# RWKV-7 attention into a SiLU layer: one ScalarE instruction for each gate, three places for w, a freer order of the weight pieces, and the scores of k in a step of their own

## The chip, the cores and the metric

The kernel runs on one core of one Trainium2 chip. The metric is the device time of one execution in microseconds. TensorE is called PE, VectorE DVE, ScalarE ACT, GpSimd POOL, and SyncE SP, as in the profile.

## What is computed

The attention part runs an RWKV-7 state over 768 tokens for 4 batches of 8 heads with 40 channels. Its output y, with the heads side by side, is the input x of a layer with 2048 hidden units:

```python
for t in range(S):
    y[:, :, t] = np.einsum('bhd,bhde->bhe', rt, state)
    Sa = np.einsum('bhde,bhe->bhd', state, at)
    state_decay = state * wt[:, :, None, :] - np.einsum('bhd,bhe->bhde', Sa, bt)
    state = state_decay + np.einsum('bhd,bhe->bhde', vt, kt)
...
h = x @ w_in
g = h * (1.0 / (1.0 + np.exp(-h)))
return (g @ w_out).astype(np.float32)
```

Everything is float32. x is 3072 x 320, w_in 320 x 2048, w_out 2048 x 320.

## The kernel before

The 768 tokens go in 12 **chunks** n of 64; the four batches form two **units** m of two batches each, so that there are 24 units k = 2n + m. Within a chunk the token recurrence is replaced by matrix products and the inverse of a lower triangular matrix. For each unit the program runs:

- **prepare** (`pre`): a running scan over w (L308) and its reciprocal (L309) on DVE, the scaling of a, b and k by them on POOL (L315, L316, L322) and two checks on ACT (L325, L326); then the scores of a and b (`pm`, L261, masked by DVE into `sb`, L269), which go to memory and come back as `mi` for the inverse. At the end of its `scores` step a unit starts the load of w for the next one (`load_w`), into the tile `w0`.
- **invert**: the inverse of the diagonal blocks, one row after another on DVE, each row a product (L380, `tmp`) and a sum (L387, `XI`). Blocks of 16 rows for chunks 0 to 3, blocks of 32 rows from chunk 4 on; from chunk 2 on two chunks are inverted at a time, during the end of the chunk before them. The result goes through memory (`xd`) to the tiles `XT`, one for each of the two chunks, which DVE transposes (L424). `merge` completes the inverse on PE (`pq`, L433 or L482, and L499).
- **chain**, which carries the state and so binds each chunk to the one before it: `keys` (transposes of k, L556 and L557), `right` (first the scores of k by `keyed`: PE L285 and the masked DVE copy L290 into `a`; then the right-hand sides `pr`, L568), `solve` (L588, L606), `read` (`pl`, L656, and the masked DVE copy `vl`, L664), `write` (`pgy`, L678 and L688; the new state `GV` by DVE L701 and L705; the output `yx`, L710, which ACT's queue sends to memory as `xs`) and `turn` (the transposed state `GT`, L631).

The hidden layer (`moe`) takes the x of two chunks. Their `xs` comes back as the tile `xt`. A step of `first` makes two 128-wide slices of h for 512 columns (256 columns for chunks 0 and 1): four calls of L753 and two of L758 into two PSUM banks `ph` of three that the layer has; ACT writes the sigmoid into `sg` (L761) and DVE multiplies (L762) into `gts`. A step of `second` is 16 calls of L767 into `po`, which DVE or ACT adds into `ot` (L776, L779). Half of the hidden units is done by eight first and four second steps, then the other half. In the trace a matmul call in float32 counts as two instructions.

The weights come in a form that the kernel makes into float32 itself, in 40 **pieces** of 256 columns: DVE steps L178, L179, L187, L189 and L190 (about 0.3 to 0.5 us each) with ACT steps L180 to L182 between them.

What sets the order: the steps of two or three lists are woven (`weave`) in proportion to their lengths, and a scheduler then orders each engine's instructions by its own estimate of times; every engine runs its list in that order. `in_order` ties an instruction to the one before it on a named line ("vector", "moe", "scalar", "sync"), so that the scheduler keeps this order. Before, the scans and reciprocals of chunks 0 to 3 and the pieces 0 to 11 are tied in the line "vector", with the rows of the first two inverses.

Of the kernel before, what the change touches and what calls it, by code (L numbers as in the profile page):

```python
# [41 lines left out]
def kernel(  # L42
# [15 lines left out]
    nc = tc.nc  # L58
# [44 lines left out]
    XI = XIf[:, 0 : 32 * 32].rearrange("p (s t) -> p s t", s=32)  # L103

    w0 = sb.tile([128, Q, C + 1], F32, name="w")
    early = [sb.tile([128, Q, C + 1], F32, name="w", tag=x, bufs=y) for x, y in (("sg", 2), ("sg", 2), ("xt", 1))]
    for w in [w0] + early:
        nc.vector.memset(w[:, :, 0:1], 0.0)
    nc.vector.memset(one, 0.0)
# [191 lines left out]
    def pre(u, md):  # L301
        def scale():
            u.W = sb.tile([128, Q, C + 1], F32, name="W", bufs=6)
            R = u.w[:, :, 1 : C + 1]
            pin = partial(in_order, line="vector") if u.n < 4 else lambda x: x
            for be in range(2):
                W, w = (x[:, P * be : P * be + P].rearrange("p q t -> p (q t)") for x in (u.W, u.w))
                pin(nc.vector.tensor_tensor_scan(W, w, one.rearrange("p q t -> p (q t)"), 0.0, ALU.mult, ALU.add))  # L308
            pin(nc.vector.reciprocal(R, u.W[:, :, 1 : C + 1]))  # L309
# [18 lines left out]
        def scores():  # L328
            if u.m == 0:
                sbs[u.n] = sb.tile([128, NM, 2, P, C], F32, name="sb", bufs=2)  # L330
            between(u, sbs[u.n][:, u.m])
            for be in range(2 if u.m == NM - 1 else 0):
                queue = nc.scalar if u.n == 1 or u.n == be == 0 else nc.sync
                for c in range(2):
                    at = 64 * (u.n % 2) + 16 * (2 * be + c)
                    r = C * be + 32 * c
                    x = send(
                        queue,
                        md[at : at + 16].rearrange("q s t -> s q t"),
                        sbs[u.n][r : r + 32, :, :, :, 32 * c : 32 * c + 32].rearrange("s m j p t -> s (m j p) t"),  # L340
                    )
                    if queue is nc.sync:
                        mark["md"] = x.ins
            k = NM * u.n + u.m + 1
            if 3 < k < NM * NN:
                load_w(units[k // NM][k % NM], w0)

        return [scale, scaled, scores] + ([keys] if u.n < 2 else [])

# [195 lines left out]
    def chain(u, xs):  # L545
# [13 lines left out]
                    behind(x, issued["scalar"])  # L559

        def right():
            keyed(u)
            pr = bank("pr")
            for p in range(P):
                for j in range(2):
# [152 lines left out]
                    y[DP * j : DP * j + D],  # L718
                )

        return [keys, right, solve, read, write] + ([] if last else [turn])


    def moe(n0, xs, apart=False):
# [19 lines left out]
        def first(T, i):  # L744
# [12 lines left out]
                R = slice(64 * n, 64 * n + 64)  # L757
                in_order(nc.tensor.matmul(ph[n], lhsT=wl_s[R, i, :], rhs=xt[R, 2, :], start=False, stop=True))  # L758
            for n in range(2):
                sg = sb.tile([128, 2 * W], F32, name="sg", bufs=2)[:, 0:N]  # L760
                nc.scalar.activation(out=sg, in_=ph[n], func=AF.Sigmoid)  # L761
                nc.vector.tensor_tensor(out=place(2 * i + n)[:, T], in0=ph[n], in1=sg, op=ALU.mult)  # L762

        def second(half, b):
            po = moe_bank("po")
# [105 lines left out]
        load_r(u)  # L871
    chains = {0: [chain(u, xs) for u in units[0]]}
    run(rows[1:18])
    run([x[i] for i in range(2) for x in chains[0]])
    run([next_steps[i] for i in (1, 2, 5, 6, 3, 7)])
    pinned(2)
    pinned(3)
# [4 lines left out]
    rows = invert(1, 1)  # L882
    run(rows[0:5] + merge0[1:2] + rows[5:9] + merge0[2:3] + rows[9:18] + merge0[3:])
    del issued["sync"]
    steps = [x for pair in zip(*[x[2:] for x in chains[0]]) for x in pair]
    steps[6:6] = late.pop(1)
    weave(steps, [partial(pinned, n) for n in range(4, 12)])
    for u in units[1]:
        load_r(u)
    for u in units[2] + units[3]:  # L890
# [1 line left out]
    fetch, queue = moe(0, xs, True)  # L892
    fetch(0)
    steps = [x for pair in zip(*[chain(u, xs) for u in units[1]]) for x in pair]
    weave(steps[0:4], convert[12:14])
    issued["moe"] = mark["right"].ins
    weave(steps[4:], queue[0:4], convert[14:21])
    del queue[0:4]
    fetch(1)
    weave(queue[0:8], prepare(2) + prepare(3) + invert(3), convert[21:31])  # L900
# [41 lines left out]
    with tc.If(flag > 0):  # L942
# [58 lines left out]
        with tc.For_i(0, B * S, 128) as t0:  # L1001
# [15 lines left out]
            for f in range(NF):  # L1017
# [58 lines left out]
```

## Time and profile before

| | us |
|---|---|
| median of three runs | 1017.0 (1015.64 to 1017.39) |
| profiled execution, whole | 1012.83 |
| its span in the trace | 1011.0 |
| PE busy | 843.2 |
| DVE busy | 648.4 |
| ACT busy | 282.3 |
| POOL busy | 128.4 |

The span falls into parts. Up to about 132 us the first chunks are prepared and the weights made, with DVE ahead of PE. From 132 to 233 us chunk 1 ends, the inverse of chunks 2 and 3 runs, and DVE is nearly always busy. From then on two kinds of stretch take turns: one in which both chunks of a pair run their chains (233 to 337 us, 408 to 484, 555 to 629, 701 to 774 and 837 to 932), and one in which DVE makes the rows of the next pair's inverse while PE has only the hidden layer to do (337 to 408, 484 to 555, 629 to 701 and 774 to 837); they are called **chain stretch** and **rows stretch**. From 932 us on PE finishes the hidden layer alone. A wait in the profile names the instruction that waited and the one whose end released it; PEld is PE's weight load, which runs beside the matmuls.

### The profile page before, as it was taken

Reading aid. Unit: us, or ns where it says so; the run is one execution under the profiler, and the core shown is the slowest. Engines: PE = TensorE matmul, PEld = TensorE weight load, DVE = VectorE, ACT = ScalarE, POOL = GpSimd, SP = SyncE. Lnnn points to the kernel's source line nnn. Section 1 sums busy time; section 2 is a strip of 40 time slices with the busy share of each in tenths; the row PEclk is TensorE's granted clock in tenths of the full one; section 3 lists DMA queues with packets and bytes.
Section 4 is the critical chain, followed back from the end, with each engine's and each line's share of the span. In section 5 each row is a group of like instructions: output and inputs, shape, how many; then the busy total and the mean of one; then the engine's idle time right before and its main releaser. Section 6 shows DMA issues by size and latency. Waiting matters only on the chain.

```text
span 1011.0 us, 25037 instructions
## 1 busy us (share of the span) xinstructions
PE 843.2 (83%) x10658; PEld 586.1 (58%) x10658; DVE 648.4 (64%) x1284; ACT 282.3 (28%) x649; POOL 128.4 (13%) x124
## 2 busy tenths in 40 slices
PE   3159689767797989998789989889989899798997
PEld 2149567446585726676526767436857357666444
DVE  9864789894466698366797285995386972721211
ACT  2314484433332121332021413022422014220210
POOL 6400032200202010103010103010111000000000
PEclk9999589995798989997889999999989999879999
DMA  7854546422434520353611344601434311302001
GB/s 146 182 129 105 151 124 156 112 73 55 95 88 92 117 62 32 67 115 88 151 33 37 68 100 103 147 21 42 105 77 86 93 31 23 73 1 71 1 0 29
DMA packets 240277, 82.96 MB, mean 82 GB/s; under 512 B 207264, under 2 KB 232096, under 8 KB 240160
## 3 DMA queue, kind: packets, MB, share of 16 engines
q1 hardware_dynamic: 219616, 69.96, 30.8%
q10 hardware_dynamic: 20544, 11.34, 4.3%
q8 instruction: 85, 1.39, 0.6%
q14 instruction: 32, 0.26, 0.1%
HBM read 67.11 MB, written 14.16 MB: 80 GB/s over the span
## 4 chain that ended last, share of the span: by engine, by line
PE 47%; DVE 29%; issue 14%; DMA 5%; ACT 2%; POOL 1%; SPq 1%; ACTq 0%; POOLq 0%; DVEq 0%
PE ph L753 10%; PE po L767 9%; DVE tmp L380 5%; DVE w L309 5%; DVE XI L387 4%; PE pl L656 4%; PE ph L758 4%; PE pr L568 3%; PE pm L285 2%; PE pq L482 2%; DVE GT L631 2%; PE pu L588 2%; PE pgy L688 2%; PE po L499 2%; DVE gts L762 2%
## 5 line engine op out<-in xcount | busy, mean ns | idle before, releaser
L753 PE MATMUL ph<-xt,wi_s 128*128 128x512 f32 (+1 forms) x448 | 206.3, 595 | 45.1 <-DVE gts L762 24.2
L767 PE MATMUL po<-wo_s,gts 128*128 128x320 f32 x768 | 219.7, 442 | 10.7 <-DVE wo_s L190 10.1
L767 PEld LDWEIGHTS po<-wo_s,gts 128*128 128x128 f32 x768 | 144.6, 192 | 75.0 <-DVE wo_s L190 10.6
L753 PEld LDWEIGHTS ph<-xt,wi_s 128*128 128x128 f32 x448 | 85.1, 206 | 136.4 <-issue 62.2
L762 DVE TENSOR_TENSOR gts<-ph,sg 128x512 f32<-128x512 f32 (+1 forms) x112 | 65.7, 604 | 101.9 <-ACT sg L761 101.7
L761 ACT ACTIVATE sg<-ph 128x512 f32<-128x512 f32 (+1 forms) x112 | 55.3, 534 | 254.4 <-PE ph L758 251.9
L380 DVE TENSOR_TENSOR tmp<-XI,mi 64x2 f32<-64x2 f32 (+40 forms) x169 | 86.0, 509 | 6.2 <-DMA mi<-md 2.4
L315 POOL TENSOR_TENSOR a<-a,W 64x512 f32<-64x512 f32 x48 | 57.2, 1192 | 250.9 <-DMA a<-in_aT 114.1
L309 DVE RECIPROCAL w<-W 128x512 f32<-128x512 f32 x24 | 80.3, 3348 | 0.6
L387 DVE TENSOR_REDUCE XI<-tmp 64x2 f32<-64x2 f32 (+40 forms) x169 | 76.2, 451 | 3.8
L568 PE MATMUL pr<-GV,a 128*64 128x40 f32 x768 | 36.9, 253 | 42.9 <-DVE a L290 25.8
L758 PE MATMUL ph<-xt,wl_s 64*128 64x512 f32 (+1 forms) x224 | 67.7, 613 | 0.0
L316 POOL TENSOR_TENSOR kb<-kb,w 128x512 f32<-128x512 f32 x24 | 29.7, 1239 | 298.2 <-DVE w L309 126.3
L568 PEld LDWEIGHTS pr<-GV,a 128*64 128x64 f32 x768 | 31.5, 161 | 59.3 <-issue 44.0
L631 DVE STREAM_TRANSPOSE GT<-GV 32x256 f32<-32x256 f32 x144 | 62.6, 435 | 2.9
L664 DVE TENSOR_TENSOR vl<-pl,ml 128x512 f32<-128x512 f32 x48 | 30.9, 685 | 47.4 <-PE pl L656 47.4
L290 DVE TENSOR_TENSOR a<-pm,ml 64x512 f32<-64x512 f32 x48 | 33.1, 689 | 37.0 <-PE pm L285 35.9
L656 PE MATMUL pl<-r,vut 64*128 64x64 f32 x768 | 54.6, 290 | 1.8 <-ACT vl L596 1.1
L656 PEld LDWEIGHTS pl<-r,vut 64*128 64x128 f32 x768 | 52.4, 203 | 4.5 <-ACT vl L596 1.9
L269 DVE TENSOR_TENSOR sb<-pm,ms 128x256 f32<-128x256 f32 x48 | 18.1, 417 | 48.5 <-PE pm L261 48.3
L261 PE MATMUL pm<-a,kb 64*64 64x64 f32 x768 | 24.6, 255 | 25.0 <-POOL kb L316 21.4
L557 ACT COPY kt<-pt 128x512 f32<-128x512 f32 x48 | 26.8, 592 | 58.1 <-DVE GV L701 37.9
(109 smaller groups left out, 1071.2 us busy)
## 6 DMA issues: line engine op xcount, KB each, us to landing
a<-in_aT SPq DMA_DIRECT2D x48, 128.0 KB
kb<-in_bT SPq DMA_DIRECT2D x48, 128.0 KB
vut<-in_vT SPq DMA_DIRECT2D x48, 128.0 KB
r<-in_rT SPq DMA_DIRECT2D x24, 256.0 KB
w<-in_wT SPq DMA_DIRECT2D x45, 128.0 KB
kb<-in_kT SPq DMA_DIRECT2D x44, 128.0 KB
vl<-in_v SPq DMA_DIRECT2D x48, 80.0 KB
xs<-yx ACTq DMA_DIRECT2D x48, 80.0 KB
```

Source lines behind the costliest of these rows:

```text
L309: pin(nc.vector.reciprocal(R, u.W[:, :, 1 : C + 1]))
L315: nc.gpsimd.tensor_tensor(out=u.a[J, j], in0=u.a[J, j], in1=u.W[J, :, 0:C], op=ALU.mult)
L380: x = nc.vector.tensor_tensor(out=part, in0=X[L, :, t + 1 : N, t + 1 : N], in1=M[L, :, t, t + 1 : N].unsqueeze(2).to_broadcast([hi - lo, I ...
L387: x = nc.vector.tensor_reduce(out=X[L, :, t + 1 : N, t], in_=part, axis=AX.X, op=ALU.add)
L568: mark["right"] = nc.tensor.matmul(pr[C * be : C * be + C, h * D : h * D + D], lhsT=u.a[:, j, P * be + p, :], rhs=gv[:, j, P * be + p, :], ...
L631: nc.vector.transpose(out=gt[T, :, 32 * e : 32 * e + 32], in_=wide[E, at : at + Q * D].rearrange("p (q d) -> p q d", q=Q)[:, :, 0:32],)
L656: nc.tensor.matmul(pl[j][:, q * C : q * C + C], lhsT=u.vut[J, q].rearrange("p n t -> p (n t)"), rhs=u.r[J, q, :], start=True, stop=True,)
L753: in_order(nc.tensor.matmul(ph[n], lhsT=wi_s[:, k, at : at + 128], rhs=xt[:, k, :], start=k == 0, stop=False))
L758: in_order(nc.tensor.matmul(ph[n], lhsT=wl_s[R, i, :], rhs=xt[R, 2, :], start=False, stop=True))
L761: nc.scalar.activation(out=sg, in_=ph[n], func=AF.Sigmoid)
L762: nc.vector.tensor_tensor(out=place(2 * i + n)[:, T], in0=ph[n], in1=sg, op=ALU.mult)
L767: in_order(nc.tensor.matmul(po[:, 0:DM], lhsT=place(f)[:, b * 128 : b * 128 + 128], rhs=wo_s[:, NF // 2 * half + f, :], start=f == 0, stop ...
```

## The change

Four things change.

- **The gate** is one ACT instruction: `Silu` from `ph` straight into `gts`. The tile `sg` and the 112 multiplies L762 are gone.
- **w** has three places in turn: `w0`, a tile that is tagged `w2`, and one that shares the tag `xt`; of the early ones two were in the place of `sg`. A load is started three units ahead, not one: unit 4 behind the scores of unit 3, units 5 to 7 behind those of unit 4.
- **The line "vector"** holds the scans and reciprocals of chunks 0 and 1 only, and no longer the pieces 4 to 11.
- **`keyed`** is a chain step of its own, so that the scores of k (L285, L290) of both units are made before `pr` of either. The indices of the woven lists move with it.

```diff
-    early = [sb.tile([128, Q, C + 1], F32, name="w", tag=x, bufs=y) for x, y in (("sg", 2), ("sg", 2), ("xt", 1))]
+    early = [sb.tile([128, Q, C + 1], F32, name="w", tag=x, bufs=y) for x, y in (("w1", 1), ("w2", 1), ("xt", 1))]
...
-            pin = partial(in_order, line="vector") if u.n < 4 else lambda x: x
+            pin = partial(in_order, line="vector") if u.n < 2 else lambda x: x
...
-            k = NM * u.n + u.m + 1
-            if 3 < k < NM * NN:
-                load_w(units[k // NM][k % NM], w0)
+            k = NM * u.n + u.m
+            for x in {3: [4], 4: [5, 6, 7]}.get(k, [k + 3] if k > 4 else []):
+                if x < NM * NN:
+                    load_w(units[x // NM][x % NM], ([w0] + early)[(x - 4) % 3])
...
         def right():
-            keyed(u)
             pr = bank("pr")
...
-        return [keys, right, solve, read, write] + ([] if last else [turn])
+        return [keys, partial(keyed, u), right, solve, read, write] + ([] if last else [turn])
...
-                sg = sb.tile([128, 2 * W], F32, name="sg", bufs=2)[:, 0:N]
-                nc.scalar.activation(out=sg, in_=ph[n], func=AF.Sigmoid)
-                nc.vector.tensor_tensor(out=place(2 * i + n)[:, T], in0=ph[n], in1=sg, op=ALU.mult)
+                nc.scalar.activation(out=place(2 * i + n)[:, T], in_=ph[n], func=AF.Silu)
...
-    run([x[i] for i in range(2) for x in chains[0]])
+    run([x[i] for i in (1, 0, 2) for x in chains[0]])
...
-    weave(steps, [partial(pinned, n) for n in range(4, 12)])
+    weave(steps, convert[4:12])
...
-    weave(steps[0:4], convert[12:14])
+    weave(steps[0:6], convert[12:14])
```

The same gate stands in the branch for inputs beyond the limits, which is not executed here. In the changed file some lines are shifted by one or two: L765 is what was L767, L381 and L388 are L380 and L387.

Since the scheduler orders anew, instructions move on all engines. Three places are shown. The first is DVE in the inverse of chunk 1, around rows 4 to 6 of 15 (`mi`, `XI` and `tmp`; `qq` belongs to the merge of chunk 0), before:

```order
L380 TENSOR_TENSOR tmp<-XI,mi 64x2x4x4
L387 TENSOR_REDUCE XI<-tmp 64x2x4
L441 TENSOR_SCALAR qq<-pq,lower 128x16x16
L380 TENSOR_TENSOR tmp<-XI,mi 64x2x5x5
L387 TENSOR_REDUCE XI<-tmp 64x2x5
L380 TENSOR_TENSOR tmp<-XI,mi 64x2x6x6
L387 TENSOR_REDUCE XI<-tmp 64x2x6
```

and after:

```order
L381 TENSOR_TENSOR tmp<-XI,mi 64x2x4x4
L187 SCALAR_TENSOR_TENSOR wo_s<-wo_s 128x256
L388 TENSOR_REDUCE XI<-tmp 64x2x4
L442 TENSOR_SCALAR qq<-pq,lower 128x16x16
L381 TENSOR_TENSOR tmp<-XI,mi 64x2x5x5
L190 TENSOR_TENSOR wi_s<-wi_s 128x256
L388 TENSOR_REDUCE XI<-tmp 64x2x5
L189 TENSOR_TENSOR wo_s<-wo_s 128x256
L381 TENSOR_TENSOR tmp<-XI,mi 64x2x6x6
```

Between two rows' instructions now stand steps of weight pieces (`wi_s`, `wo_s`, `wl_s`, `room`); before, the pieces stood behind the last row. The second place is DVE at the end of chunk 5, where the rows for chunks 6 and 7 begin and the last output of the chunk (`yx`, L710) is made. Before:

```order
L380 TENSOR_TENSOR tmp<-XI,mi 128x1
L705 TENSOR_TENSOR GV_90<-GV_90,W 64x320
L387 TENSOR_REDUCE XI<-tmp 128x1
L779 TENSOR_TENSOR ot_4575<-po,ot_4575 128x320
L380 TENSOR_TENSOR tmp<-XI,mi 128x2x2
L631 STREAM_TRANSPOSE GT_91<-GV_89 32x8x32
L387 TENSOR_REDUCE XI<-tmp 128x2
L631 STREAM_TRANSPOSE GT_91<-GV_89 32x8x32
L380 TENSOR_TENSOR tmp<-XI,mi 128x3x3
L710 TENSOR_TENSOR yx<-pgy,W 128x4x64
L387 TENSOR_REDUCE XI<-tmp 128x3
L710 TENSOR_TENSOR yx<-pgy,W 128x4x64
```

and after:

```order
L381 TENSOR_TENSOR tmp<-XI,mi 128x13x13
L701 TENSOR_TENSOR GV_90<-pgy,GV_90 64x160
L388 TENSOR_REDUCE XI<-tmp 128x13
L701 TENSOR_TENSOR GV_90<-pgy,GV_90 64x160
L381 TENSOR_TENSOR tmp<-XI,mi 128x14x14
L705 TENSOR_TENSOR GV_90<-GV_90,W 64x320
L388 TENSOR_REDUCE XI<-tmp 128x14
L705 TENSOR_TENSOR GV_90<-GV_90,W 64x320
L381 TENSOR_TENSOR tmp<-XI,mi 128x15x15
L710 TENSOR_TENSOR yx<-pgy,W 128x4x64
L388 TENSOR_REDUCE XI<-tmp 128x15
L710 TENSOR_TENSOR yx<-pgy,W 128x4x64
```

The last L710 stood among the first four rows; now it stands behind row 15. The third place is PE from the last `pl` of chunk 5 to the first step of the hidden layer for chunks 4 and 5. Before:

```order
L656 MATMUL pl<-r,vut_96 128x64 x16
L678 MATMUL pgy<-r,GT_91 64x64 x16
L688 MATMUL pgy<-vl,kt 64x104 x16
L678 MATMUL pgy<-r,GT_92 64x64 x16
L688 MATMUL pgy<-vl,kt 64x104 x16
L767 MATMUL po<-wo_s,gts 128x320 x12
L753 MATMUL ph<-xt,wi_s 128x512 x4
```

and after:

```order
L656 MATMUL pl<-r,vut_96 128x64 x16
L678 MATMUL pgy<-r,GT_91 64x64 x16
L688 MATMUL pgy<-vl,kt 64x104 x16
L765 MATMUL po<-wo_s,gts 128x320 x8
L678 MATMUL pgy<-r,GT_92 64x64 x16
L688 MATMUL pgy<-vl,kt 64x104 x16
L765 MATMUL po<-wo_s,gts 128x320 x16
L753 MATMUL ph<-xt,wi_s 128x512 x4
```

Ahead of that first step there are now 24 calls of the second product (`po`) behind the last `pl`, where there were 12.

## Rows read from the trace of the kernel before

**Rows 1.** Stretches: length, busy per engine, granted PE clock, DMA share, GB/s.

```profile
62.00:132.00 70.00, 51.87 (x1262) 49.21 (x1262) 46.64 (x123) 29.83 (x69) 4.42 (x6) 0.83 0.51 125
132.00:233.00 101.00, 78.08 (x824) 56.60 (x824) 90.76 (x205) 48.97 (x129) 23.22 (x18) 0.92 0.48 119
233.00:337.00 104.00, 85.21 (x1896) 71.54 (x1898) 54.08 (x109) 34.66 (x84) 16.21 (x16) 0.78 0.35 82
337.00:408.00 71.00, 64.44 (x312) 34.93 (x309) 61.96 (x119) 12.36 (x26) 4.92 (x4) 0.95 0.29 70
408.00:484.00 76.00, 70.02 (x1240) 53.12 (x1238) 40.94 (x71) 25.34 (x57) 13.99 (x12) 0.93 0.42 92
484.00:555.00 71.00, 59.41 (x293) 32.38 (x292) 61.13 (x115) 11.00 (x23) 4.90 (x4) 0.90 0.28 71
555.00:629.00 74.00, 70.01 (x1239) 52.59 (x1238) 41.29 (x72) 25.92 (x58) 13.98 (x12) 0.93 0.42 92
629.00:701.00 72.00, 63.27 (x315) 35.13 (x314) 61.76 (x117) 10.78 (x23) 4.89 (x4) 0.95 0.34 74
701.00:774.00 73.00, 67.14 (x1247) 50.88 (x1245) 41.80 (x74) 25.62 (x58) 14.02 (x12) 0.95 0.39 83
774.00:837.00 63.00, 58.28 (x313) 33.84 (x310) 51.17 (x110) 7.71 (x14) 0.00 (x0) 0.97 0.29 69
837.00:932.00 95.00, 86.67 (x1261) 63.20 (x1259) 33.20 (x67) 23.34 (x51) 0.00 (x0) 0.89 0.17 40
```

**Rows 2.** Waits of PE, whole span: total us, times, longest.

```profile
PE ph L753 <- DMA xt<-xs: 19.9, 5, 6.3
...
PE pr L568 <- issue: 12.9, 5, 5.2
```

**Rows 3.** Groups by form on VectorE and ScalarE: count, busy, mean ns, idle before.

```profile
L309 DVE RECIPROCAL w<-W 128x512 f32<-128x512 f32 x24 | 80.3, 3348 | 0.6
...
L762 DVE TENSOR_TENSOR gts<-ph,sg 128x512 f32<-128x512 f32 x80 | 53.5, 682 | 92.9 <-ACT sg L761 92.6
...
L308 DVE TENSOR_TENSOR_SCAN W<-w,one 128x260 f32<-128x260 f32 x48 | 33.2, 707 | 5.6 <-DMA w<-in_wT 5.5
...
L762 DVE TENSOR_TENSOR gts<-ph,sg 128x256 f32<-128x256 f32 x32 | 12.2, 409 | 9.0 <-ACT sg L761 9.0
...
L187 DVE SCALAR_TENSOR_TENSOR room<-room 128x256 int32<-128x256 int32 x17 | 8.1, 477 | 4.3 <-ACT room L180 4.3
...
L761 ACT ACTIVATE sg<-ph 128x512 f32<-128x512 f32 x80 | 44.5, 596 | 224.0 <-PE ph L758 223.9
```

**Rows 4.** Timeline of VectorE, 60 to 132 us: start, duration, work, idle before.

```profile
91.24 1.29 DVE L664 TENSOR_TENSOR vl<-pl,ml 128x512 f32<-128x512 f32 x2 [9.91 <-PE pl L656]
```

**Rows 5.** Waits of PE from 132 to 233 us.

```profile
PE ph L753 <- DVE gts L762: 8.7, 5, 3.0
PE po L767 <- DVE wo_s L190: 5.7, 1, 5.7
```

**Rows 6.** Timeline from 484 us, end of chunk 5: VectorE and PE.

```profile
484.46 1.29 DVE L664 TENSOR_TENSOR vl<-pl,ml 128x512 f32<-128x512 f32 x2 [0.50 <-PE pl L656]
...
489.67 6.73 PE L767 MATMUL po<-wo_s,gts 128*128 128x320 f32 x24
...
495.17 0.42 DVE L710 TENSOR_TENSOR yx<-pgy,W 128x256 f32<-128x256 f32 x1
...
502.72 1.22 PE L753 MATMUL ph<-xt,wi_s 128*128 128x512 f32 x1 [6.32 <-DMA xt<-xs]
...
504.21 0.26 DVE L387 TENSOR_REDUCE XI<-tmp 128x10 f32<-128x100 f32 x1
```

**Rows 7.** The 20 us behind the wait of group 6, columns as in group 1.

```profile
502.00:522.00 20.00, 14.82 (x26) 5.34 (x27) 19.51 (x33) 3.11 (x8) 2.41 (x2) 0.70 0.27 67
```

**Rows 8.** The page, fifth part: first-product matmuls: count, busy, mean ns, idle before.

```profile
L753 PE MATMUL ph<-xt,wi_s 128*128 128x512 f32 (+1 forms) x448 | 206.3, 595 | 45.1 <-DVE gts L762 24.2
...
L758 PE MATMUL ph<-xt,wl_s 64*128 64x512 f32 (+1 forms) x224 | 67.7, 613 | 0.0
```

More of the change, by code (lines that the diff above doesn't have):

```diff
@@ L884 @@
     del issued["sync"]
-    steps = [x for pair in zip(*[x[2:] for x in chains[0]]) for x in pair]
+    steps = [x for pair in zip(*[x[3:] for x in chains[0]]) for x in pair]
     steps[6:6] = late.pop(1)
-    weave(steps, [partial(pinned, n) for n in range(4, 12)])
+    weave(steps, convert[4:12])
     for u in units[1]:
@@ L894 @@
     steps = [x for pair in zip(*[chain(u, xs) for u in units[1]]) for x in pair]
-    weave(steps[0:4], convert[12:14])
+    weave(steps[0:6], convert[12:14])
     issued["moe"] = mark["right"].ins
-    weave(steps[4:], queue[0:4], convert[14:21])
+    weave(steps[6:], queue[0:4], convert[14:21])
     del queue[0:4]
@@ L910 @@
         steps = [x for pair in zip(*[chain(u, xs) for u in units[n]]) for x in pair]
-        steps[4:4] = late.pop(n, [])
+        steps[6:6] = late.pop(n, [])
         now = 8 if n > 2 else 4
-        weave(steps[0:4], queue[0 : now // 4], convert[31:34] if n == 2 else [])
-        weave(steps[4:], queue[now // 4 : now], prepare(n + 2) + invert(n + 2), convert[34:] if n == 2 else [])
+        weave(steps[0:6], queue[0 : now // 4], convert[31:34] if n == 2 else [])
+        weave(steps[6:], queue[now // 4 : now], prepare(n + 2) + invert(n + 2), convert[34:] if n == 2 else [])
         del queue[0:now]
@@ L1024 @@
                 nc.tensor.matmul(ph[:, 0:128], lhsT=wl_s[R, f // 2, :], rhs=xg[R, 2], start=False, stop=True)
-                nc.scalar.activation(out=gg[:, f], in_=ph[:, 0:128], func=AF.Sigmoid)
-                nc.vector.tensor_tensor(out=gg[:, f], in0=ph[:, 0:128], in1=gg[:, f], op=ALU.mult)
+                nc.scalar.activation(out=gg[:, f], in_=ph[:, 0:128], func=AF.Silu)
             po = gps.tile([128, 512], F32, name="gpo")
```

## The prediction, made before the changed kernel ran

> **What bounds the kernel now.** I read the busy time by stretches first, then what ended PE's waits in each, then the instructions themselves. The stretches show who sets the pace [rows 1]. From 132 to 233 us DVE is busy for 90.76 of 101 us and PE for 78.08: DVE leads. In a rows stretch both are nearly full (337 to 408 us: PE 64.44, DVE 61.96 of 71). In a chain stretch PE leads (408 to 484 us: 70.02 of 76) and DVE has room (40.94). Length less PE's busy time, over the ten stretches from 132 to 932 us, is 97 us: about the most that can go there. Of PE's waits in the whole span 24.2 us are for the gate's multiply [rows 8], 19.9 for `xt`, and 12.9 stand ahead of `pr` with no releaser named [rows 2]. So an instruction that leaves DVE counts in full from 132 to 233 us, and later by the waits of PE that it ends.
>
> **The gate.** ACT's pass exists already and takes 596 ns on 512 columns; the multiply behind it takes 682 ns, 80 times, and 409 ns on 256 columns, 32 times: 53.5 + 12.2 = 65.7 us leave DVE [rows 3]. No row has Silu. Its lower bound is the Sigmoid row; the upper one is two such passes, 1.19 us, on an engine that is busy for 49 of 101 us at its fullest behind 132 us [rows 1]. I take the Sigmoid row, since one instruction takes the place of one on the same tile; the sum counts no gain on ACT. A `ph` bank also comes free without DVE's queue.
>
> A rule speaks against it: the Trainium skill ("ScalarE: Activation LUTs", Rules for kernel authors) wants a multiplication on VectorE, not on ScalarE. By it the pair of instructions would stay, and the sum would lose what the gates give. No run here shows a multiplication by itself on ACT; the rows show one pass there with or without it, so I go by the rows.
>
> **Up to 132 us.** Ahead of chunk 1's L290, DVE gets in addition 4 scans (0.71 us), 2 reciprocals (3.35) and 11 steps of pieces (0.48 by L187): 2.8 + 6.7 + 5.3 = 14.8 us [rows 3]. DVE is idle for 70 - 46.64 = 23.4 us there [rows 1], 9.91 of them in one wait for `pl` [rows 4], and that idle time is the cover; without it the 14.8 us would be paid in full. The steps between the rows of chunk 1 make those rows end later, but ahead of that wait. Bounds -3 to +15; I take **+3**, nearest to the idle row.
>
> **From 132 to 233 us.** Between chunk 1's L290 and the last row of chunks 2 and 3, 22 multiplies (9.0 us by 0.409), 2 reciprocals (6.7), 4 scans (2.8) and 7 steps of pieces (3.3) are gone: 21.8 us of DVE's work [rows 3], in a stretch that DVE leads. PE stops this before all is won: it is idle there for 101 - 78.08 = 22.9 us, of which 8.7 us are for the gate and 5.7 for a weight piece [rows 5], 14.4 together. Bounds -5 to -21; I take **-16**, a little over those 14.4.
>
> **From 233 to 337 us.** PE's clock is only 0.78 here, against 0.92 and 0.95 beside it, and 104 - 85.21 = 18.8 us are idle [rows 1]. At 0.95 the busy time would be 85.21 x 0.78 / 0.95 = 70 us, so -15 is one end; none is the other. With DVE ready earlier I take **-6**.
>
> **The rows stretches.** Three things change in each.
> - DVE loses the multiplies: 8.3, 6.1, 6.8 and 5.5 us (13, 9, 10 and 8 of them, two of the first 13 on 256 columns) [rows 3]. From the second stretch on one or two additions of `ot` come in from elsewhere, about 0.5 us.
> - PE loses work to the chain stretches. A call of L767 takes 6.73 / 12 = 0.56 us [rows 6], one of L753 2 x 206.3 / 448 = 0.92, one of L758 2 x 67.7 / 224 = 0.60 [rows 8]. From the last `pl` to the first `pq` the calls of L767 go from 48, 44, 51, 52 to 48, 52, 48, 29, those of L753 from 25, 21, 22, 18 to 23, 16, 16, 16, those of L758 from 13, 10, 10, 8 to 10, 8, 8, 8. That is 3.6, 1.3, 8.4 and 14.7 us less, 28 in all.
> - The last L710 of an odd chunk comes later, because the rows now begin before it and stand among its steps. In chunk 5 it started 10.7 us behind the first L664, and PE's first step of the next hidden layer followed 7.6 us behind it, after a wait of 6.32 us [rows 6]. Of the rows, 3, 3, 4 and 4 stood ahead of that L710; now 6, 15, 18 and 19 do. A row costs about 0.52 us (the sum of row 10 takes 0.26 [rows 6], its product as much); with some `turn` and `ot` steps that moved along, L710 comes later by 3.6, 8.0, 7.8 and 7.4 us. What covers this on PE grows less: by 12 calls of L767 (6.7 us) in the second stretch, 5 and 4 (2.8, 2.2) in the next two, 2.7 us in the first. So PE's waits for `xt` grow by 0.9, 1.3, 5.0 and 5.2 us, from 19.9 [rows 2] to about 32 us.
>
> PE's time for a stretch is then its length less the work that left, plus that growth, less some 4 us of waits for the gate in each of the first three (24.2 [rows 8] less 8.7 [rows 5] lie behind 233 us): 64.3, 67, 64.6 and 53.5 us. DVE's is the length less the multiplies and plus the additions: 63, 66, 65.5 and 58. The later of the two, against 71, 71, 72 and 63 us [rows 1], gives -6.7, -4, -6.5 and -5: **-22**. The ends are 0 and -30.
>
> **The chain stretches** of chunks 4 to 11 get the 28 us of PE's work. They have 6.0, 4.0, 5.9 and 8.3 us of idle PE, 24.2 in all [rows 1]; half as much, 12.9 us, stands ahead of `pr` [rows 2], where `keyed` as a step lets the second unit's scores be made while the first's are masked. I let half be filled: **+16**. The ends are +28 (nothing filled) and +4 (all).
>
> **w.** The earlier loads end waits of DVE's scans for w, 5.5 us in all [rows 3], in stretches that PE's work covers; without that cover they would be worth those 5.5 us. I take nothing. From 932 us on PE is alone at work: nothing as well.
>
> **The sum** is +3 - 16 - 6 - 22 + 16 = -25 us. On the profiled execution's own time, 1012.83, it gives 987.8. The median of the runs is 4.2 us above that execution, so the forecast is 1017 - 25 = **992 us**.
>
> **Rivals.**
> 1. *The start gives nothing back.* The pieces among the rows of chunk 1 hold up the chain there, and the 14.8 us are paid. Then -13 in all: 1004 us. For it: rows that now wait behind pieces on an engine that runs in order. Against it: the 9.91 us of idle time behind them [rows 4].
> 2. *All of PE's waits go.* The chain stretches fill all 24.2 us (+4 for +16), the start reaches its -21 and the clock its -15: -25 - 12 - 5 - 9 = -51, 966 us. For it: DVE loses a tenth of its work, and PE waited 24.2 us for the gate alone [rows 8]. Against it: the waits for `xt`, which grow.
> 3. *Slower: the rows hold up the write.* The rows of the inverse, begun early, delay L710 and with it `xt`, and PE stands in all four rows stretches. After the wait of 6.32 us the clock was 0.70 for 20 us [rows 7], where such a stretch has 0.95 [rows 1]: 14.82 x (1 - 0.70 / 0.95) = 3.9 us. If longer waits cost that in all four (+16) and eat the whole -22, the sum is +3 - 16 - 6 + 0 + 16 + 16 = +13: 1030 us. It decides from the point where the rows stretches, clock included, grow by 3 us together instead of shrinking by 22. For it: DVE's order, in which the output's last step stands behind row 15. Against it: both engines have less to do there.
>
> Beside the third: the Trainium skill ("TensorE: Matmul & The Clock Gate", HAM oscillation) says that a matmul kernel whose engine stands for a transfer again and again falls to the slow clock each time. The 0.70 behind the 6.32 us [rows 7] agrees.
>
> **How the numbers follow.** The forecast (980 to 1000 us) gets 0.46, the first rival 0.17, the second 0.20, the third 0.15, anything else 0.02. About 0.2% is what a measurement can tell from no change. Faster: the forecast, the second and nearly all of the first, 0.80; the same, between the first and the third, 0.05; slower 0.15. The range leaves out the lower third of the second and the upper part of the third: 960 to 1021 us.
>
> **What would show it.** Right: no DVE work on `gts`; the last row of chunks 2 and 3 some 10 to 15 us earlier; rows stretches of 58 to 67 us, with waits for `xt` of 8 to 9 us in the last three; chain stretches of chunks 4 to 11 longer by 2 to 7 us; fewer microseconds ahead of `pr`. Wrong: an ACT pass of Silu far over 0.6 us, L664 of chunk 0 far behind 91 us, rows stretches that don't shrink, or a granted clock under 0.8 in them.

## The result: 991 us, 2.9% less

The changed kernel takes 990.98 us (median of its runs, 983.11 to 1001.77), the kernel before 1017.19 us beside it; the ratio is 0.971, with a 95% interval of 0.9637 to 0.9783. In a second measurement of six runs, a2 below, it was 0.9652 (0.9596 to 0.9708). The ratios leave out every execution over 1.5% slower than the fastest of its kernel, three of the six in a2; the median of all six, 986.97 us, is 0.971 of the kernel before's. The forecast was 992 us. Its profiled execution took 988.55 us, with a span of 986.5.

The page's first part, after:

```profile
PE 826.7 (84%) x10658; PEld 577.4 (59%) x10658; DVE 593.9 (60%) x1172; ACT 281.1 (28%) x649; POOL 132.8 (13%) x124
```

DVE has 112 instructions and 54.5 us less; the 112 multiplies had taken 65.7 us [rows 3], and where the other 11 us went was not followed. The gates by form, on ACT (count, busy, mean ns, idle before):

```profile
L760 ACT ACTIVATE gts<-ph 128x512 f32<-128x512 f32 x80 | 43.8, 593 | 229.4 <-PE ph L758 229.4
L760 ACT ACTIVATE gts<-ph 128x256 f32<-128x256 f32 x32 | 10.7, 380 | 23.5 <-PE ph L758 22.3 <-DVE wo_s L178 1.2
```

Silu takes 593 ns where Sigmoid took 596 [rows 3].

For the stretches I take the same events as ends: chunk 1's L290, the first `pq` of chunk 2, the last `pl` of each odd chunk and the first `pq` of the next even one. In the kernel before they lie at 132, 231, 337, 408, 484, 555, 629, 701, 774 and 835 us, close to the ends of [rows 1]. After (length, busy per engine, granted PE clock, DMA share, GB/s):

```profile
0.00:129.65 129.65, 59.86 (x1568) 55.94 (x1568) 119.66 (x234) 51.91 (x122) 39.66 (x48) 0.89 0.65 152
129.65:214.60 84.95, 73.62 (x786) 54.74 (x787) 66.66 (x155) 43.14 (x114) 16.66 (x12) 0.94 0.52 127
214.60:311.20 96.60, 78.86 (x1892) 66.95 (x1893) 52.50 (x105) 34.28 (x84) 16.34 (x16) 0.77 0.36 82
311.20:379.10 67.90, 57.76 (x292) 33.20 (x290) 58.04 (x106) 10.36 (x23) 5.21 (x4) 0.96 0.37 85
379.10:456.50 77.40, 72.34 (x1244) 52.95 (x1244) 36.48 (x64) 27.03 (x60) 14.20 (x12) 0.90 0.40 87
456.50:520.50 64.00, 54.73 (x283) 31.94 (x282) 55.76 (x107) 8.95 (x20) 6.05 (x4) 0.97 0.35 83
520.50:603.80 83.30, 77.77 (x1258) 56.30 (x1258) 37.60 (x72) 27.33 (x61) 13.96 (x12) 0.90 0.41 87
603.80:665.60 61.80, 53.89 (x274) 30.76 (x272) 54.03 (x100) 9.27 (x20) 6.50 (x4) 0.94 0.30 73
665.60:753.50 87.90, 83.28 (x1266) 60.77 (x1268) 37.95 (x74) 27.44 (x61) 14.24 (x12) 0.84 0.33 70
753.50:805.80 52.30, 43.16 (x234) 23.65 (x235) 44.46 (x93) 5.31 (x9) 0.00 (x0) 0.93 0.28 72
805.80:986.50 180.70, 171.47 (x1576) 110.21 (x1576) 30.75 (x64) 36.05 (x76) 0.00 (x0) 0.98 0.12 28
```

| part | before, us | after, us | difference | forecast |
|---|---|---|---|---|
| up to chunk 1's L290 | 132.1 | 129.65 | -2.4 | +3 |
| to the first `pq` of chunk 2 | 98.8 | 84.95 | -13.9 | -16 |
| to the last `pl` of chunk 3 | 106.0 | 96.6 | -9.4 | -6 |
| four rows stretches | 70.7, 70.4, 71.2, 61.2 | 67.9, 64.0, 61.8, 52.3 | -27.5 | -22 |
| chain stretches from chunk 4 on, with the end | 76.8, 74.6, 73.1, 176.1 | 77.4, 83.3, 87.9, 180.7 | +28.7 | +16 |

In these two profiles the whole saving is made by 337 us of the old time. Behind that the rows stretches win 27.5 us and the chain stretches lose 28.7: their PE is busy for 72, 78 and 83 us where it was busy for 70, 70 and 67 [rows 1], at a lower clock.

PE's waits, after (total us, times, longest; the first lies in the start):

```profile
PE pt L557 <- DVE a L290: 23.0, 1, 23.0
...
PE ph L753 <- DMA xt<-xs: 14.1, 3, 6.1
PE pq L483 <- DVE XT L425: 11.8, 4, 4.3
PE pm L261 <- POOL a L315: 8.7, 5, 2.1
PE po L765 <- DVE wo_s L190: 7.4, 1, 7.4
PE pr L568 <- DVE a L290: 6.4, 9, 2.1
```

The waits for the gate's multiply, 24.2 us before [rows 8], are gone; 9.4 us of waits for the gate's ACT pass have come (5.6 at `ph`, 3.8 at `po`). New behind the start are those at `pq` (L483), where PE waits for DVE's transposes of `XT`: PE has no work left in its order ahead of `pq` at the end of the rows stretches.

### The profile page after: what moved, and what is told of

Read it like the earlier page. It is cut to its first block, busy times and chain, and to the rows that moved or that the text cites. A ratio compares the mean times of both kernels' runs of the same rounds, so it can differ in the third digit from the quotient of the medians.

```text
span 986.5 us, 24857 instructions
## 1 busy us (share of the span) xinstructions
PE 826.7 (84%) x10658; PEld 577.4 (59%) x10658; DVE 593.9 (60%) x1172; ACT 281.1 (28%) x649; POOL 132.8 (13%) x124
## 5 line engine op out<-in xcount | busy, mean ns | idle before, releaser
L765 PE MATMUL po<-wo_s,gts 128*128 128x320 f32 x768 | 226.5, 451 | 11.2 <-DVE wo_s L190 7.4
L753 PE MATMUL ph<-xt,wi_s 128*128 128x512 f32 (+1 forms) x448 | 201.3, 586 | 30.5 <-DMA xt<-xs 14.1
L765 PEld LDWEIGHTS po<-wo_s,gts 128*128 128x128 f32 x768 | 146.3, 195 | 76.5 <-DVE wo_s L190 7.9
L753 PEld LDWEIGHTS ph<-xt,wi_s 128*128 128x128 f32 x448 | 84.8, 204 | 113.7 <-issue 66.4
L760 ACT ACTIVATE gts<-ph 128x512 f32<-128x512 f32 (+1 forms) x112 | 54.5, 532 | 252.9 <-PE ph L758 251.6
L381 DVE TENSOR_TENSOR tmp<-XI,mi 64x2 f32<-64x2 f32 (+40 forms) x169 | 81.8, 484 | 7.9 <-DMA mi<-md 3.9
L388 DVE TENSOR_REDUCE XI<-tmp 64x2 f32<-64x2 f32 (+40 forms) x169 | 76.2, 451 | 4.2
L664 DVE TENSOR_TENSOR vl<-pl,ml 128x512 f32<-128x512 f32 x48 | 31.1, 686 | 70.3 <-PE pl L656 63.2
L777 DVE TENSOR_TENSOR ot<-po,ot 128x320 f32<-128x320 f32 x24 | 11.7, 486 | 93.4 <-PE po L765 82.6
L290 DVE TENSOR_TENSOR a<-pm,ml 64x512 f32<-64x512 f32 x48 | 33.1, 689 | 54.8 <-PE pm L285 53.6
L758 PE MATMUL ph<-xt,wl_s 64*128 64x512 f32 (+1 forms) x224 | 60.8, 601 | 0.0
L557 PE MATMUL pt<-ident,kb 128*128 128x128 f32 x192 | 36.3, 351 | 25.8 <-DVE a L290 23.0
L656 PEld LDWEIGHTS pl<-r,vut 64*128 64x128 f32 x768 | 46.3, 189 | 5.2 <-issue 2.1
L557 PEld LDWEIGHTS pt<-ident,kb 128*128 128x128 f32 x192 | 29.9, 182 | 33.0 <-issue 23.5
L656 PE MATMUL pl<-r,vut 64*128 64x64 f32 x768 | 48.0, 274 | 0.1
L483 PE MATMUL pq<-XT,sb 32*32 32x32 f32 x768 | 29.8, 209 | 17.8 <-DVE XT L425 11.8
```

The costliest lines, as they stand in the source:

```text
L290: x = nc.vector.tensor_tensor(out=u.a[O, j], in0=pm[O].rearrange("p (q t) -> p q t", q=Q), in1=ml[O].unsqueeze(1).to_broadcast([C, Q, C]), ...
L381: x = nc.vector.tensor_tensor(out=part, in0=X[L, :, t + 1 : N, t + 1 : N], in1=M[L, :, t, t + 1 : N].unsqueeze(2).to_broadcast([hi - lo, I ...
L388: x = nc.vector.tensor_reduce(out=X[L, :, t + 1 : N, t], in_=part, axis=AX.X, op=ALU.add)
L557: nc.tensor.transpose(out=pt[:, c : c + 128], in_=u.kb[:, q].rearrange("p n t -> p (n t)"), identity=ident)
L656: nc.tensor.matmul(pl[j][:, q * C : q * C + C], lhsT=u.vut[J, q].rearrange("p n t -> p (n t)"), rhs=u.r[J, q, :], start=True, stop=True,)
L753: in_order(nc.tensor.matmul(ph[n], lhsT=wi_s[:, k, at : at + 128], rhs=xt[:, k, :], start=k == 0, stop=False))
```

## The experiments

The ratios below are to the kernel before, run on the same chip in the same hour, with 95% intervals. For the profiles I give two times, which split each run: the last `pl` of chunk 5, and from there to the first `pq` of chunk 10, called the **steady part** (three rows stretches and the two chain stretches between them). Each of these parts comes from one profile of each kernel; how far such profiles differ stands below the table.

### One part of the change alone

e1_silu_alone puts Silu into the kernel before, and gives the early tiles of w tags of their own, since `sg` is gone:

```diff
-                sg = sb.tile([128, 2 * W], F32, name="sg", bufs=2)[:, 0:N]
-                nc.scalar.activation(out=sg, in_=ph[n], func=AF.Sigmoid)
-                nc.vector.tensor_tensor(out=place(2 * i + n)[:, T], in0=ph[n], in1=sg, op=ALU.mult)
+                nc.scalar.activation(out=place(2 * i + n)[:, T], in_=ph[n], func=AF.Silu)
```

> The kernel before with Silu as the one change (the early tiles of w get tags of their own, since the sigmoid's tile is gone). Theory 'the start': 9 of the 21.8 us that leave DVE between 132 and 233 us are gates, so half the gain there, 1002 to 1009 us. Rival 'the gates alone': the whole gain, 989 to 996 us.

Measured: 980.08 us, ratio 0.9672 (0.9632 to 0.9712).

e8_pins_alone puts the freer order into the kernel before:

```diff
-            pin = partial(in_order, line="vector") if u.n < 4 else lambda x: x
+            pin = partial(in_order, line="vector") if u.n < 2 else lambda x: x
...
-    weave(steps, [partial(pinned, n) for n in range(4, 12)])
+    weave(steps, convert[4:12])
```

> The kernel before with the freer order as the one change: scans and reciprocals of chunks 2 and 3 and the pieces 4 to 11 are not tied. Theory 'the start': the other half, 1005 to 1011 us. Rival 'the gates alone': 1014 to 1020 us.

Measured: 1008.82 us, ratio 0.994 (0.9911 to 0.997).

So the gate alone is worth as much as the whole change; the freer order alone is worth 0.6%. e8 lies in the range of the theory 'the start', e1 outside both of its ranges, 9 us below the rival's. Up to the last `pl` of chunk 3 the profiles show 14 us less for Silu alone, 6.5 for the order alone and 26 for the whole change: the gates bring more there than the order, not half. Silu alone also wins 25 us behind that point, where the prediction had given the whole change 6. Its steady part, by stretches:

```profile
464.00:531.00 67.00, 58.95 (x286) 32.98 (x286) 57.24 (x107) 10.77 (x23) 5.05 (x4) 0.95 0.34 78
531.00:603.50 72.50, 67.40 (x1254) 49.84 (x1256) 36.75 (x66) 25.59 (x58) 13.96 (x12) 1.00 0.44 95
603.50:670.50 67.00, 59.19 (x288) 32.91 (x289) 57.28 (x107) 10.75 (x23) 5.05 (x4) 0.95 0.34 78
670.50:744.00 73.50, 68.26 (x1250) 51.06 (x1250) 37.61 (x66) 25.83 (x58) 14.02 (x12) 0.98 0.38 83
```

A rows stretch is 67 us in place of 71 [rows 1], with DVE 4 us less busy, and the chain stretches are not longer than before. In the changed kernel the rows stretches are shorter still, 64.0 and 61.8, but a chain stretch takes 83.3 and 87.9.

### Taking a part back

Three kernels have the whole change but for one part. e4_pins_back ties scans, reciprocals and pieces again (the diff of e8 the other way):

> The changed kernel with scans and reciprocals of chunks 2 and 3 and the pieces 4 to 11 tied again in DVE's line. Theory 'the start': about half the gain goes, 1000 to 1006 us. Rival 'the gates alone': 988 to 994 us.

Measured: 989.96 us, ratio 0.979 (0.9736 to 0.9843), in the range of the rival 'the gates alone'.

e3_keyed_back makes the scores of k in `right` again (the indices of the woven lists go back with it):

```diff
         def right():
+            keyed(u)
...
-        return [keys, partial(keyed, u), right, solve, read, write] + ([] if last else [turn])
+        return [keys, right, solve, read, write] + ([] if last else [turn])
```

> The changed kernel with the scores of k made as the first part of the right-hand sides again, unit by unit. Theory of the prediction: the step of its own ends part of PE's waits ahead of the right-hand sides in the chain stretches, so without it the time is 4 to 10 us longer, 995 to 1002 us. Rival: the chain stretches are full of the hidden layer's work anyway, and it is the same within 3 us, 988 to 994 us.

Measured: 994.58 us, ratio 0.9786 (0.9734 to 0.9837). The time lies between the two expected ranges. Both intervals overlap with that of the first measurement of the whole change (0.9637 to 0.9783), but not with that of a2 (0.9596 to 0.9708); what each part adds is not to be told from these two.

e5_w_back loads w one unit ahead, into `w0`, as before:

```diff
-            k = NM * u.n + u.m
-            for x in {3: [4], 4: [5, 6, 7]}.get(k, [k + 3] if k > 4 else []):
-                if x < NM * NN:
-                    load_w(units[x // NM][x % NM], ([w0] + early)[(x - 4) % 3])
+            k = NM * u.n + u.m + 1
+            if 3 < k < NM * NN:
+                load_w(units[k // NM][k % NM], w0)
```

> The changed kernel with w loaded one unit ahead into one place, as before. Both theories: the earlier loads lie beside PE's work, so this stays within 3 us of the changed kernel, 988 to 994 us; if the waits of the scans for w (5.5 us before) had been on the path, 994 to 998 us. It is also the kernel against which the next three stand, which all load w in this way.

Measured: 1001.44 us, ratio 0.987 (0.983 to 0.991). That is outside both ranges: it lost more than the waits for w can explain, 5.5 us [rows 3].

### Gates in one half only, all with w one unit ahead

e6_silu_first and e7_silu_later choose by the layer (shown is e6; e7 has `if not apart`); e2_no_silu has the pair, Sigmoid and multiply, everywhere:

```diff
+                if apart:
                     nc.scalar.activation(out=place(2 * i + n)[:, T], in_=ph[n], func=AF.Silu)
+                else:
+                    sg = sb.tile([128, 2 * W], F32, name="sg", bufs=2)[:, 0:N]
+                    nc.scalar.activation(out=sg, in_=ph[n], func=AF.Sigmoid)
+                    nc.vector.tensor_tensor(out=place(2 * i + n)[:, T], in0=ph[n], in1=sg, op=ALU.mult)
```

> As e5_w_back, with Silu only in the hidden layer of chunks 0 and 1 (32 gates of 256 columns) and the pair of instructions in all later ones. Theory 'the start': nearly the whole gain stays, 991 to 999 us, since later stretches are bounded by PE. Rival 'the waits later' (the 15.5 us of PE's waits for the gate behind 233 us are the gain): 1003 to 1010 us.

Measured: 995.9 us, ratio 0.9761 (0.9705 to 0.9816).

> As e5_w_back, with Silu only in the hidden layers of chunks 2 to 11 (80 gates of 512 columns) and the pair of instructions in the first. Theory 'the start': as without Silu, less some 5 us, 998 to 1006 us. Rival 'the waits later': 990 to 996 us, as with Silu everywhere.

Measured: 991.81 us, ratio 0.9782 (0.9743 to 0.9822).

> As e5_w_back, but every gate is again a Sigmoid on ACT and a multiply on DVE: only the freer order of the pieces and the step of its own for the scores of k are left of the change. Theory 'the start' (the gain is made up to 337 us, where DVE leads, about half of it by gates and half by scans and pieces that moved into idle time): 1003 to 1010 us. Rival 'the gates alone' (the order brings nothing): 1014 to 1020 us.

Measured: 1001.61 us, ratio 0.9847 (0.9795 to 0.99).

Silu everywhere (e5, 0.987) is no faster here than Silu nowhere (0.9847). Silu in either half is faster than Silu everywhere, and faster than none by the medians alone (the intervals of e6 and e7 overlap with that of e2). e6 came out as the theory 'the start' had it and e7 as its rival had it, so neither holds; e2 came 1.4 us below the theory's range. On this base the parts don't add up, so something other than the gates' own time moves with them. The order does: the scheduler puts the same hidden-layer calls elsewhere.

e2 also shows a gain without Silu, 1.5%. It differs from e8 by the step of its own for the scores of k, with its indices, and the intervals of the two, measured on different chips, don't overlap (0.9795 to 0.99, 0.9911 to 0.997): where there is no Silu, that step is worth about 0.9%.

### What moved with the parts

The table counts, in PE's order, the calls of L753, L758 and L767 in the chain stretches of chunks 6/7 and 8/9, at the prices of [rows 6, 8], and sets them beside lengths from one profile each: the two chain stretches together, the rows stretches of chunks 5, 7 and 9 together, and their sum, the steady part. A row counts as ahead of L710 when its product is. The last four kernels have the pair in the later layers.

| kernel | hidden-layer work in two chain stretches, us | rows ahead of the last L710 (chunks 5, 7, 9) | last `pl` of chunk 5 | two chain stretches, us | three rows stretches, us | steady part, us |
|---|---|---|---|---|---|---|
| e7_silu_later | 42 | 6, 6, 9 | 471.1 | 146 | 190 | 335.9 |
| k9_after_rows5 (below) | 42 | 5, 5, 6 | 459.8 | 151 | 192 | 343.1 |
| e1_silu_alone | 45 | 3, 3, 2 | 464.0 | 146 | 191 | 336.9 |
| k3_silu_pins (below) | 45 | 3, 3, 2 | 455.0 | 150 | 191 | 341.2 |
| e3_keyed_back | 48 | 10, 13, 16 | 470.5 | 160 | 187 | 347.5 |
| k8_after_rows3 (below) | 52 | 3, 3, 3 | 455.6 | 163 | 192 | 354.7 |
| changed kernel | 55 | 15, 18, 19 | 456.5 | 171 | 178 | 349.3 |
| changed kernel, profile of a2 | 55 | 15, 18, 19 | 460.8 | 171 | 178 | 348.3 |
| e4_pins_back | 55 | 15, 18, 19 | 462.8 | 164 | 178 | 341.7 |
| e5_w_back | 55 | 8, 15, 12 | 469.3 | 163 | 188 | 351.0 |
| before | 41 | 3, 4, 4 | 484.4 | 148 | 203 | 350.5 |
| e8_pins_alone | 41 | 3, 4, 4 | 482.1 | 149 | 204 | 352.8 |
| e2_no_silu | 38 | 5, 5, 5 | 476.9 | 147 | 207 | 354.7 |
| e6_silu_first | 38 | 5, 5, 5 | 467.5 | 150 | 209 | 358.6 |

How far two profiles can differ is seen where the order behind the last `pl` of chunk 5 is the same: the changed kernel's two profiles and e4 have 349.3, 348.3 and 341.7 us in the steady part. A difference under 8 us between two profiles therefore says nothing.

By kinds of stretch the kernels separate. The two chain stretches take 146 to 151 us where up to 45 us of hidden-layer work stand in them, with Silu or without, and 160 to 171 us where 48 to 55 do (one order alone, that of the changed kernel and e4, gives 164 to 171). The three rows stretches take 203 to 209 us with the pair in the later layers, 187 to 192 with Silu there, and 178 in the three profiles in which 15 and more rows stand ahead of the last L710. In the changed kernel the gain and the loss nearly cancel: 25 us less than before in the rows stretches, 24 more in the chain stretches.

Two things could lengthen the steady part: that the rows begin early and hold up the write, as in the third rival, or that PE has lost its work ahead of `pq`. The next two kernels were made to tell them apart.

k8_after_rows3 is the whole change, with empty steps that hold the fourth row back and a tie behind L710, which is all that differs (k9_after_rows5: the same with the first row):

```diff
+            if N == 32 and t == 27:
+                behind(x, mark["yx"])
...
+        more = invert(n + 2)
+        if more:
+            more = more[0 : 4] + [lambda: None] * 70 + more[4:]
-        weave(steps[6:], queue[now // 4 : now], prepare(n + 2) + invert(n + 2), convert[34:] if n == 2 else [])
+        weave(steps[6:], queue[now // 4 : now], prepare(n + 2) + more, convert[34:] if n == 2 else [])
```

> The whole change, with the fourth row of each later inverse tied behind the last L710, so that three rows stand ahead of it in all four stretches; PE then has 26 us of the hidden layer in the later chain stretches and 48 in the rows stretches, nearly as in the changed kernel. Theory 'the write is held up': the steady part takes 337 to 342 us, 973 to 980 us in all. Rival 'the work that moved' (what counts is that PE has too little left of the hidden layer ahead of pq and so waits there and loses its clock): 345 to 350 us, 983 to 991 us in all.

Measured: 997.12 us, ratio 0.9848 (0.9795 to 0.9902); steady part 354.7 us.

> The whole change, with the first row of each later inverse tied behind the last L710 of the first unit or later by the order of the program: 2, 5, 5 and 6 rows stand ahead of the last L710, and PE keeps 54 us of the hidden layer in the rows stretches of chunks 5 to 8 (52 with Silu alone, 46 to 49 in the changed kernel). Both theories: the steady part takes 336 to 342 us, 970 to 978 us in all. If neither order nor moved work is the cause, but the loads of w or the scores of k, it stays at 347 to 351 us and 985 to 993 us in all.

Measured: 981.06 us, ratio 0.9661 (0.9609 to 0.9712); steady part 343.1 us.

k8 lies above the ranges of both theories, k9 1 to 3 us above its range. Their whole times differ clear of noise (0.9795 to 0.9902, 0.9609 to 0.9712). k9's steady part lies within the spread of the changed kernel's order, and its interval overlaps with both of the changed kernel's. Rows stretch and chain stretch of k8, then of k9:

```profile
455.60:523.80 68.20, 55.12 (x282) 32.26 (x281) 58.18 (x107) 9.38 (x20) 4.66 (x4) 0.92 0.37 86
523.80:607.30 83.50, 77.58 (x1258) 55.74 (x1258) 37.25 (x70) 27.19 (x61) 14.17 (x12) 0.90 0.41 86
```

```profile
459.80:527.50 67.70, 59.11 (x294) 34.51 (x294) 57.76 (x107) 9.82 (x21) 5.15 (x4) 0.97 0.37 87
527.50:606.70 79.20, 73.01 (x1244) 52.82 (x1246) 36.47 (x64) 26.64 (x60) 13.96 (x12) 0.89 0.39 85
```

In k8 PE has 4 us less to do in a rows stretch, and the stretch is no shorter: DVE, about as busy in both, sets it. It has 4.6 us more to do in the chain stretch, which is 4.3 us longer. Over both chain stretches k8 takes 12 us more; the busy times times the granted clock are 139.6 us (77.58 x 0.90 + 74.20 x 0.94) and 131.1 us (73.01 x 0.89 + 67.49 x 0.98), so by this estimate some 8.5 of the 12 us are work.

k8 is no test of the held-up write, though. Three rows stand ahead of its last L710, but other DVE work, scans and a reciprocal among it, stands there instead, and the write starts as late as in the changed kernel. First DVE's L664 and last L710 of chunk 5 in the changed kernel, then in k8, where the lines are L666 and L712:

```profile
456.61 1.29 DVE L664 TENSOR_TENSOR vl<-pl,ml 128x512 f32<-128x512 f32 x2 [1.49 <-PE pl L656]
...
473.15 0.41 DVE L710 TENSOR_TENSOR yx<-pgy,W 128x256 f32<-128x256 f32 x1
```

```profile
455.72 1.29 DVE L666 TENSOR_TENSOR vl<-pl,ml 128x512 f32<-128x512 f32 x2 [1.50 <-PE pl L658]
...
473.07 0.76 DVE L712 TENSOR_TENSOR yx<-pgy,W 128x256 f32<-128x256 f32 x2
```

What speaks against the held-up write is where the time goes. The third rival lets PE wait for the write in the rows stretches. These are as long in k8 as in k9 although PE's first step there waits 7.0 and 7.2 us in k8 and 4.3 and 4.8 us in k9. They are shortest of all in the changed kernel. So the rows that begin early are a gain of some 13 us there, which k8 gives up (178 to 192 us); the loss is in the chain stretches, with the moved work, and k8 keeps it.

### Two parts together, and the changed kernel again

k3_silu_pins joins the edits of e1 and e8:

> The kernel before with two parts of the change: Silu and the freer order of scans, reciprocals and pieces; w and the scores of k as before. In DVE's order three rows of the inverse stand ahead of the last L710, as in the kernel before (in the changed kernel 7, 15, 18 and 19). Theory 'the write is held up' (the rows that start early take back in the steady part what the start has won): the start of the changed kernel and the steady part of Silu alone, 336 to 341 us from the last pl of chunk 5 to the first pq of chunk 10 (349.3 in the changed kernel), 966 to 974 us in all. Rival 'chance of the clock' (the steady part differs by when the clock falls, whatever the order): 980 to 990 us.

Measured: 980.9 us, ratio 0.9676 (0.9632 to 0.972). The start (last `pl` of chunk 5 at 455.0) and the steady part (341.2) came as the theory had them, but the whole time lies in the range of the rival 'chance of the clock': from chunk 10's `pq` to the end it takes 177.2 us, Silu alone 171.1 and the changed kernel 180.7. The freer order adds nothing to Silu that can be measured in the whole. Behind the last `pl` of chunk 5 the two kernels have the same order but for four of PE's instructions; the granted clock differs. The chain stretch of chunks 6 and 7 (531.0 to 603.5 us of Silu alone, above) and the end in k3, then the end of Silu alone:

```profile
522.00:599.20 77.20, 72.29 (x1252) 52.62 (x1252) 36.68 (x64) 25.81 (x58) 13.99 (x12) 0.93 0.40 89
796.20:973.40 177.20, 164.94 (x1528) 104.28 (x1528) 30.89 (x64) 34.83 (x73) 0.00 (x0) 0.93 0.12 28
```

```profile
800.90:972.00 171.10, 159.31 (x1528) 100.09 (x1528) 30.91 (x64) 34.52 (x73) 0.00 (x0) 0.98 0.13 29
```

In these two profiles k3's gain at the start goes where its clock is lower, 0.93 against 1.00 and 0.98.

> The changed kernel itself once more, in as many rounds as the other kernels, so that they can be set against it. If the work that moved costs it part of the gain (the steady part 8 to 12 us longer than with Silu alone), its ratio to the kernel before is 0.975 to 0.982, with e4_pins_back, whose later order is the same; Silu alone has 0.967. If Silu alone is no faster than the whole change, it is 0.965 to 0.970.

Measured: 986.97 us as a median of all six runs (975.29 to 999.61), and 0.9652 (0.9596 to 0.9708). The ratio is in the range expected if Silu alone is no faster than the whole change, so a loss against it can't be told in the whole time. The changed kernel's single runs lie further apart, 975 to 1000 us against 974 to 984 us.

## Why the prediction was right, and where it was not

- **What bounds it, the gate, the first parts.** Right. The price of Silu was that of Sigmoid. L664 of chunk 0 started at 89.82 us behind 1.47 us of idle time instead of 9.91 [rows 4]: the pieces did go into that gap, so the first rival's 14.8 us were not paid, and the start was 2.4 us shorter, not 3 longer. From there to the first `pq`, -13.9 for -16. To the last `pl` of chunk 3, -9.4 for -6, without the clock's help, which stayed at 0.77.
- **The rows stretches**, -27.5 for -22. DVE's side was right in sum: its busy time fell by 23 us in the four, where the prediction took some 25 off. One by one they came to -2.8, -6.4, -9.4 and -8.9 for -6.7, -4, -6.5 and -5, and the first and the last, 67.9 and 52.3 us, lie outside the 58 to 67 that was given as a sign. PE's waits for `xt` were put too high: 5.2, 4.9, 5.6 and 6.1 us, where 8 to 9 were expected for the last three. (The middle two stand in the waits under a DVE instruction; in a2's profile the same matmul waits 5.5 and 5.8 us for `xt`.) The last L710 of chunk 5 started 16.5 us behind the L664 of the last `pl`, not 10.7 + 8, and PE's step followed 6.9 us behind that.
- **The chain stretches**, +28.7 for +16: this term was mis-sized, and its step that failed is "I let half be filled". They grew by 0.6, 8.7, 14.8 and, with the end, 4.6 us, where 2 to 7 were expected of each. The waits ahead of `pr` did go as that step had it: from chunk 4 on they were 12.1 us without a releaser and 2.5 for `a`, and are 2.9. But PE got new ones at `pq` (11.8 us for `XT`, 1.3 before) and more at `pm` for POOL (9.7 us, 3.7 before), and ran at a lower clock. The chain stretches before, between the same events:

```profile
407.60:484.40 76.80, 70.78 (x1252) 53.84 (x1252) 41.19 (x71) 25.46 (x58) 13.99 (x12) 0.93 0.42 91
554.80:629.40 74.60, 70.60 (x1246) 53.12 (x1246) 41.49 (x72) 25.92 (x58) 13.98 (x12) 0.93 0.42 92
700.60:773.70 73.10, 67.23 (x1243) 50.98 (x1245) 41.90 (x74) 25.62 (x58) 14.02 (x12) 0.95 0.39 83
834.90:1011.00 176.10, 160.99 (x1519) 102.91 (x1518) 45.48 (x87) 34.29 (x72) 0.00 (x0) 0.94 0.12 28
```

  Against the four after, PE's busy time grew by 35.3 us and its idle time fell by 6.6. Busy time times clock, stretch by stretch, grew by about 26 us. By this estimate the 28.7 are the moved work, nearly in full, plus 9 us of a lower clock, less 7 us of idle time that was filled, where 12 were counted on. In the chain stretch from 520.5 us alone it is 77.77 x 0.90 = 70.0 us, and 67.40 x 1.00 = 67.4 us in that of Silu alone: 2.6 of the 10.4 us that PE is busier are work, about 7.8 are the clock. The two mistakes, -5.5 and +12.7, and those of the start, about -7, left a sum that was right by luck as much as by its steps.
- **Who earns it.** The forecast gave the order of scans and pieces more of the start than the gates (12.8 of 21.8 us), and the later gates little. Silu alone had the whole gain; from the last `pl` of chunk 5 to the first `pq` of chunk 10 it won 13.6 us, and with the pair in the later layers instead of Silu (e6 against e7, one base) that part was 22.7 us longer, though the ratios of these two, 0.9761 and 0.9782, don't differ. An instruction taken from DVE counts in every rows stretch, since DVE sets their length: 191 us for 203, Silu alone against before.
- **w** was taken at nothing. (Its three places are `w0` and the tiles tagged `w1` and `w2`; the one that shares the tag `xt` is used at the start alone.) e5 is 1.6% slower than the changed kernel, but its order differs too, so the loads' own price stays open.
- **The third rival** described what DVE's order shows, rows ahead of L710, and L710 did come later. But the rows stretches, which it wanted longer, are the shortest of all kernels, at a clock of 0.93 to 0.97. What the early rows came with, work moved from the rows stretches to the chain stretches, goes with longer chain stretches in every kernel of the table. A kernel that has the write early and the work moved was not made.

## What to carry to other kernels

Take an instruction from the engine that sets the length of a stretch, and look at once at which filler the scheduler moves out of that stretch: filler that leaves a stretch bounded by another engine comes back in full where its own engine is the bound. Measure each part of a joint change alone; here one part of four had all of the gain, and on another base the same part had none. With a scheduler that orders anew, compare the orders too: here they sorted the stretches by length, though not the whole times.

## What the runs showed of the hardware

In the chain stretches of the changed kernel PE's clock fell to its lower level behind waits of 1.8 to 4.3 us that stand right ahead of the first small matmuls (`pq`). In chunks 6 and 7 it waited 3.69 us for `XT` until 520.49 us, and the five microseconds each from 515 on read:

```profile
515.00:520.00 5.00, 1.79 (x7) 0.95 (x5) 0.35 (x1) 0.45 (x2) 0.00 (x0) 1.00 0.49 142
520.00:525.00 5.00, 4.51 (x38) 3.50 (x39) 1.75 (x3) 0.58 (x1) 0.00 (x0) 0.60 0.43 68
525.00:530.00 5.00, 4.93 (x61) 2.87 (x61) 0.00 (x0) 1.00 (x2) 0.00 (x0) 0.71 0.00 0
530.00:535.00 5.00, 5.00 (x72) 4.63 (x74) 0.00 (x0) 3.31 (x6) 0.00 (x0) 0.66 0.01 3
535.00:540.00 5.00, 5.00 (x139) 4.08 (x135) 3.46 (x5) 0.74 (x3) 0.00 (x0) 1.00 0.36 82
```

Shares of 0.60 to 0.71 are a mixture of its two levels, 1.2 and 2.4 GHz. The clock fell again behind two waits of 2.1 and 1.8 us ahead of `pm` (0.75 and 0.57 from 580 and 585 us on). Such waits don't settle it alone. It also fell where PE had been busy without a gap, in chunks 8 and 9:

```profile
685.00:690.00 5.00, 5.00 (x85) 3.63 (x82) 0.00 (x0) 2.15 (x4) 4.65 (x4) 0.50 0.40 90
690.00:695.00 5.00, 5.00 (x90) 4.18 (x88) 0.00 (x0) 3.61 (x10) 0.00 (x0) 0.50 0.57 123
```

Silu alone came through the place in chunks 6 and 7, with a wait of 1.7 us, at 1.00 (its chain stretch above); k3, with a wait of 1.7 us and nearly the same order, ran it at 0.93. And with one order the changed kernel, its profile in a2 and e4 ran the chain stretch of chunks 8 and 9 at 0.84, 0.88 and 0.94. So neither the wait nor the order settles the fall; no experiment here held the clock up, and the 9 us of the chain stretches that are put down to it above are an estimate.
